# Attention and maxout kernel, batch 0: scores before row sums, the cast of v before the inverses, and four w2 transposes before the last values

## The chip, the cores and the metric

The kernel runs on one core of a Trainium2 chip. The metric is device time in microseconds (us) of one execution, as a median over runs. The engines have their own instruction queues and run side by side: TensorE (PE, with its weight loads shown as PEld), VectorE (DVE), ScalarE (ACT), GpSimd (POOL) and SyncE (SP). Each engine executes its own queue in order, and engines wait for one another on semaphores. Matmul results go to PSUM, which here is cut into four single banks and two pairs of banks.

## The reference

```python
def _attn_ref(q, k, v, E, F):                       # q, k, v: 8 x 8 x 1024 x 64; E, F: 64 x 1024
    k_proj = np.einsum('ks,bhsd->bhkd', E, k)
    v_proj = np.einsum('ks,bhsd->bhkd', F, v)
    scale = 1.0 / np.sqrt(q.shape[-1])
    scores = scale * np.matmul(q, k_proj.transpose(0, 1, 3, 2))
    scores = scores - np.max(scores, axis=-1, keepdims=True)
    attn = np.exp(scores)
    attn = attn / (np.sum(attn, axis=-1, keepdims=True) + 1e-09)
    return np.matmul(attn, v_proj)

def _moe_ref(x, w1, w2, w_out):                     # x: 8192 x 512; w1, w2: 512 x 1024; w_out: 1024 x 512
    h1 = x @ w1
    h2 = x @ w2
    g = np.maximum(h1, h2)
    return g @ w_out
```

The heads of the attention output are joined into x, and the second part runs on it. The kernel uses max(h1, h2) = relu(x (w1 - w2)) + x w2, so it needs the difference `wd_sb` = w1 - w2, and the product m = w2 w_out, for which w2 is transposed once (`w2t_sb`).

## The kernel before, in words

Work goes by batch (8 of them). In a batch k and v are projected to 64 rows per head, the scores of 8 heads are taken in four groups (g, j): g names four heads, j a half of the 512 positions that one tile holds. A group passes these steps, each a function that appends instructions to the engines' queues:

- `step_sc`: 16 score matmuls on PE (line 340) into a pair of banks, then one Exp on ACT (line 380) to `ex_sb`.
- `step_dn`: 8 matmuls with ones on PE (line 352), which write the row sums into the same pair of banks, then one Ln on ACT (line 388) to `ld_sb`.
- `step_inv`: one Exp(-x) on ACT (line 427), which turns the Ln into the inverse sums in place, and a small DMA of a few rows on SP's queue (line 396) for a later range check.
- `step_at`: 16 value matmuls on PE (line 352), and two products with the inverse on DVE (line 443), which write `xt_sb`.

`step_kv(..., "v")` projects v for some heads (line 195) and casts the result to `vp_sb` (line 207), on DVE or, for heads 4 to 8, on ACT. That last call takes two heads, then runs what is given as `between`, then takes the other two heads; both halves lie in one bank of a pair.

For batch 0 the second part has no saved sums yet. An up block (`up_slots`, line 525) is four accumulating matmuls of `wd_sb` with `xt_sb` into one single bank, then a relu on ACT or DVE. The blocks `u0[0]`, `u0[1]`, `u1[0]`, `u1[1]` are cut into a first half (`r1=2`, which needs only group g = 0) and a second half (`r0=2`, which needs g = 1); `u0` needs j = 0 and `u1` needs j = 1. `step_wd` (line 541) makes pieces of `wd_sb` on DVE. `step_w2t` turns 256 columns of w2 with eight transposes on PE (line 557) into one bank, and copies them to `w2t_sb` with ACT (line 563).

The order on every engine is the order of the calls (`tc.manual_schedule()`): nothing is moved by a scheduler. The four single banks are handed out in turn from the list `turn` (`mm_bank`); the two pairs alternate with each call of `att_banks`, so that each call waits until the pair of two calls ago has been read for the last time. The call of `att_banks()` alone only advances that alternation. The lines around the change are 979 to 1005 and the list `slots`, which orders the work after them.

In this order the pairs are taken so: scores (1,0) take a pair, which their row sums share; scores (1,1) take the other pair; v of heads 4 to 8 takes the first pair again; the values (1,0) take the first pair once more and the values (1,1) the second. The values (0,0) and (0,1) take the four single banks.

Of the kernel before, what the change touches and what calls it, by code (L numbers as in the profile page):

```python
# [10 lines left out]
FP16 = mybir.dt.float16  # L11
# [8 lines left out]
def kernel(  # L20
# [12 lines left out]
    nc = tc.nc  # L33
# [8 lines left out]
    NDC = DM // 128  # L42
# [20 lines left out]
    turn = [0, 1, 2, 3]  # L63

    def mm_bank(dtype=FP32, n=None):
        if n is None:
            n = turn.pop(0)
            turn.append(n)
        return ps.tile([128, 512 if dtype == FP32 else 1024], dtype, tag=f"mm{n}", name="mm_ps")

    def att_banks(dtype=FP32):
        return ps.tile(
            [128, 2, 512 if dtype == FP32 else 1024], dtype, tag="att", bufs=2, name="att_ps"
        )
# [108 lines left out]
    def step_kv(t, h0=0, h1=H, which="kv", att=False, dma=False, copy=nc.vector.tensor_copy, between=None):  # L183
        kv_ps = att_banks()[:, 0, :] if att else mm_bank(n=0 if dma else None)
        n = (h1 - h0) * D
        both = which == "v"
        nh = 2 if both else h1 - h0
        for h in range(0, h1 - h0, nh):
            if h and between is not None:
                between()  # L190
            for c in range(NC):
                for w in which:
                    i = "kv".index(w)
                    for r in range(2) if both else (i,):
                        nc.tensor.matmul(  # L195
                            out=kv_ps[r * KP : (r + 1) * KP, h * D : (h + nh) * D],
                            lhsT=eft[i][:, c, :],
                            rhs=t[w][:, h0 + h : h0 + h + nh, c, :],
                            start=(c == 0), stop=(c == NC - 1),
                        )  # L200
        zd = lambda ap: ap.rearrange("p (h d z) -> p h z d", d=D // 2, z=2)
        if "k" in which:
            eng = nc.vector.tensor_copy if which == "k" or dma else nc.scalar.copy
            kp = t["kp"][:, h0:h1]
            eng(out=kp[:, :, 0, :], in_=kv_ps[0:KP, 0:n].rearrange("p (h d) -> p h d", d=D))
        if both:
            copy(out=t["vp"][:, h0:h1], in_=zd(kv_ps[:, 0:n]))
        elif "v" in which:
            def finish_v():
                nc.vector.tensor_copy(out=t["vp"][KP:128, h0:h1], in_=zd(kv_ps[KP:128, 0:n]))  # L210
                if dma:
                    nc.vector.tensor_copy(out=kp[:, :, 1, :], in_=kp[:, :, 0, :])
                    step_kpt_dma(t)
                else:
                    step_vp(t, h0, h1)

            if att:
                return finish_v
            finish_v()


    def step_vp(t, h0=0, h1=H):
        fl = lambda ap: ap[:, h0:h1].rearrange("p h z d -> p (h z d)")
        nc.vector.tensor_copy(out=fl(t["vp"][0:KP]), in_=fl(t["vp"][KP:128]))
# [71 lines left out]
    def step_kpt_dma(t):  # L296
        nc.sync.dma_start_transpose(
            out=t["kpt"], in_=t["kp"].rearrange("p h r d -> p (h r d)")
        )
# [33 lines left out]
    def score(t, g, j, banks):  # L333
        for h in range(2):
            for o in range(2):
                for e in range(2):
                    head = 4 * g + 2 * h + e
                    for s in range(2):
                        pos = D * (o ^ e) + s * Z
                        nc.tensor.matmul(  # L340
                            out=banks[e][pos : pos + Z, h * W : (h + 1) * W],
                            lhsT=kpt_of(t, head, o)[:, s * Z : (s + 1) * Z],
                            rhs=t["qt"][o * D : (o + 1) * D, head, j * W : (j + 1) * W],
                            start=True, stop=True,
                        )
        t["ex", g, j] = soft.tile([128, 2, HALF], FP16, tag="soft", name="ex_sb")
# [12 lines left out]
    def sums_into(t, g, j, dn_ps):  # L359
        tiles_into(lambda o: dn_ps[:, o, :], t["ex", g, j], lambda rows, hh: ones16[rows, 0:Z])  # L360

    def values_into(t, g, j, at_ps):
        for z in range(2):
            tiles_into(
                lambda o: at_ps[o][:, z * W : (z + 1) * W], t["ex", g, j],
                lambda rows, hh: vp_of(t, 4 * g + hh, rows, z),
            )

    def new_xt(t):
        t["xt"] = xpool.tile([128, NP2, 2, HALF], FP16, tag="xt", name="xt_sb")  # L370

    def x_out(t, g, j):
        return t["xt"][:, 2 * g : 2 * g + 2, :, j * W : (j + 1) * W]


    def step_sc(t, g, j):
        sc_ps = att_banks()
        t["ps", g, j] = sc_ps
        score(t, g, j, [sc_ps[:, e, :] for e in range(2)])
        nc.scalar.activation(out=t["ex", g, j], in_=sc_ps, func=ACTF.Exp, scale=scale)  # L380

    def step_dn(t, g, j):
        dn_ps = t.pop(("ps", g, j))[:, :, 0:W]
        sums_into(t, g, j, dn_ps)
        ld = (ppool.tile([128, 2, W], FP32, tag="pd", bufs=4, name="ld_sb") if t is tiles[0]
              else soft.tile([128, 2, W], FP32, tag="soft", name="ld_sb"))
        t["ld", g, j] = ld
        nc.scalar.activation(out=t["ld", g, j], in_=dn_ps, func=ACTF.Ln)  # L388
# [4 lines left out]
    def check(inv):  # L393
        rows = checked[4 * n_checked[0] : 4 * n_checked[0] + 4, :]
        n_checked[0] += 1
        nc.sync.dma_start(
            out=rows, in_=inv.rearrange("(a z) o w -> a z (o w)", z=Z)[:, 0, :]
        )
# [26 lines left out]
    def step_inv(t, g, j):  # L425
        ld = t["ld", g, j]
        nc.scalar.activation(out=ld, in_=ld, func=ACTF.Exp, scale=-1.0)
        check(ld)

    def step_at(t, g, j, att=False, between=None):  # L430
        if "xt" not in t:
            new_xt(t)
        ld = t.pop(("ld", g, j))
        if att:
            both = att_banks()
            at_ps = [both[:, o, :] for o in range(2)]
        else:
            at_ps = [mm_bank() for _ in range(2)]
        values_into(t, g, j, at_ps)
        for o in range(2):  # L440
            if o and between is not None:
                between()
            nc.vector.tensor_tensor(
                out=x_out(t, g, j)[:, :, o, :],
                in0=at_ps[o].rearrange("q (z n) -> q z n", z=2),
                in1=ld[:, o, None, :].broadcast_to([128, 2, W]),
                op=ALU.mult,
            )
# [101 lines left out]
                out=rows(wd_sb), in0=rows(w1_sb), in1=rows(w2_sb), op=ALU.subtract  # L550
            )

    def step_w2t(f0, att=False):
        ps_t = att_banks(FP16)[:, 0, :] if att else mm_bank(FP16)
        for f in range(2):
            for r in range(NDC):
                nc.tensor.transpose(
                    out=ps_t[:, (f * NDC + r) * 128 : (f * NDC + r + 1) * 128],
                    in_=w2_sb[:, r, f0 + f * 128 : f0 + (f + 1) * 128],
                    identity=ident16,  # L560
                )
        fb = f0 // 128
        nc.scalar.copy(
            out=w2t_sb[:, fb : fb + 2, :].rearrange("q f m -> q (f m)"), in_=ps_t
        )
# [390 lines left out]
    t = tiles[0]  # L956
# [27 lines left out]
    step_sc(t, 1, 0)  # L984
    step_kv(t, 0, 2, "v")
    step_kv(t, 2, 4, "v")
    step_dn(t, 1, 0)
    step_sc(t, 1, 1)
    step_at(t, 0, 0)
    step_at(t, 0, 1)  # L990
    step_inv(t, 1, 0)
    step_kv(t, 4, 8, "v", True, copy=nc.scalar.copy, between=lambda: step_dn(t, 1, 1))
    step_inv(t, 1, 1)
    att_banks()
    for f0 in (0, 128):
        step_wd(f0, 0, 2, 128)
    step_at(t, 1, 0, True)
    u0, u1 = [*up_slots(t, 0)], [*up_slots(t, 1)]
    step_wd(0, 2, 4)
    step_at(t, 1, 1, True)  # L1000
    first_banks = turn[0:2], turn[2:4]
    for i in range(2):
        for u in u0, u1:
            u[i](r1=2)
    step_w2t(0, True)


    load_all(tiles[1], 1, "k", k)
# [4 lines left out]
    def loads(b, *names):  # L1013
# [15 lines left out]

    slots = [  # L1030
        (0, lambda: u0[0](r0=2)), (1, lambda: u0[1](r0=2)), (None, lambda: loads(1, "v", "q", "k")),
        (None, lambda: step_w2t(256, True)),
        (2, lambda: u1[0](r0=2)), (3, lambda: u1[1](r0=2)),
        (None, wd[1]), (4, u0[2]), (5, u0[3]),
        (None, wd[2]), (6, u1[2]), (7, u1[3]), (None, wt[2]), (None, wt[3]), (8, u0[4]), (9, u0[5]), (None, wd[3]),
# [45 lines left out]
    t = tiles[1]  # L1081
# [29 lines left out]
    t = tiles[2]  # L1111
# [8 lines left out]
    for b in range(3, B):  # L1120
        t = tiles[b]
        n = 2 * b - 3
# [13 lines left out]
    for i, (new, old) in enumerate(zip([*groups[1:], none], groups)):  # L1136
        n, h = divmod(i + 2, 2)
# [9 lines left out]
    for n, (b, o) in enumerate(units):  # L1147
        u = U[b, o]
# [33 lines left out]
    for key, slot in slots:  # L1182
        r = slot()
        pending = [g for g in [r, *(f() for f in pending)] if g is not None]
        for s in steps.pop(key, ()):
            r = s()
# [177 lines left out]
```

## Time and profile before

| | us |
|---|---|
| median of three runs (lowest, highest) | 319.72 (319.67, 319.75) |
| the profiled execution, its own time | 320.29 |
| its span in the trace | 318.5 |
| PE busy | 311.8 (98% of the span) |
| DVE busy | 241.1 (76%) |
| ACT busy | 206.0 (65%) |
| POOL busy | 41.4 (13%) |

A row of the timeline reads: start and duration in us, engine, line, operation, destination and source, shape, count; in brackets the idle time of the engine before it and what ended it. Rows of matmuls include the time that the last one needs to pass through the array, so rows that follow each other overlap. A row of the waits reads: engine, destination and line that waited, what it waited for, then total us, times, and longest. Times of the trace count from the start of the span.

### The profile page before, as it was taken

How to read it: one execution, taken by the hardware profiler on the slowest of the kernel's cores; microseconds unless marked ns; L12 is line 12 of the kernel's file. 1: busy time of each engine (PE TensorE's matmuls, PEld its weight loads, DVE VectorE, ACT ScalarE, POOL GpSimd, SP SyncE). 2: the span in 40 equal slices, each digit the busy share in tenths (PEclk: the TensorE clock that was granted, in tenths of full speed). 3: DMA queues.
4: the chain of work that ended last, by engine and by line, in shares of the span. 5: the costliest groups of instructions: out<-in, count | busy, mean ns of one | idle time of the engine just before them, and what ended most of it. 6: DMA issues, size and time to landing. Idle time of an engine off the chain costs nothing.

```text
span 318.5 us, 9309 instructions
## 1 busy us (share of the span) xinstructions
PE 311.8 (98%) x3922; PEld 253.8 (80%) x3922; DVE 241.1 (76%) x442; ACT 206.0 (65%) x373; POOL 41.4 (13%) x63
## 2 busy tenths in 40 slices
PE   7999999999999999999999999999999999999996
PEld 3565588888887888788887888788887888888885
DVE  2366889887969696896969696996969696969883
ACT  2386742777776777477776777477776777765541
POOL 8259102004000300012000400030000000000000
PEclk9999999999999999999999999999999999999999
DMA  7999999999989999799999999989979131313124
GB/s 179 206 202 197 207 207 201 207 156 141 204 163 183 171 209 245 208 188 147 225 229 219 169 199 245 221 155 174 230 153 217 42 101 36 102 35 102 36 99 136
DMA packets 76684, 53.71 MB, mean 169 GB/s; under 512 B 29664, under 2 KB 76128, under 8 KB 76640
## 3 DMA queue, kind: packets, MB, share of 16 engines
q0 software_dynamic: 30688, 28.05, 56.0%
q1 hardware_dynamic: 45664, 24.85, 33.1%
q8 instruction: 31, 0.51, 0.6%
q10 hardware_dynamic: 288, 0.20, 0.2%
q14 instruction: 13, 0.11, 0.1%
HBM read 57.15 MB, written 16.78 MB: 232 GB/s over the span
## 4 chain that ended last, share of the span: by engine, by line
PE 95%; DMA 3%; ACT 1%; DVE 1%; issue 0%; POOLq 0%
PE mm_ps L838 47%; PE mm_ps L746 27%; PE mm_ps L525 4%; PE mm_ps L195 4%; PE att_ps L352 4%; PE mm_ps L340 2%; DMA k_sb<-in_k_dram 2%; PE mm_ps L634 2%; PE att_ps L237 1%; PE mm_ps L311 1%; PE mm_ps L153 1%; DMA out_dram<-o_sb 1%; PE att_ps L340 0%; DVE qt_sb L316 0%; ACT ld_sb L388 0%
## 5 line engine op out<-in xcount | busy, mean ns | idle before, releaser
L720 ACT COPY p_sb<-mm_ps 128x512 f32<-128x512 f32 x179 | 101.7, 592 | 49.2 <-PE mm_ps L746 27.3
L838 PEld LDWEIGHTS <-big 128*128 128x128 f16 x768 | 73.5, 98 | 11.8 <-issue 3.6
L838 PE MATMUL mm_ps<-T_sb,big 128*128 128x256 f16 x576 | 76.9, 273 | 0.0
L761 DVE TENSOR_TENSOR gt_sb<-mm_ps,p_sb 128x512 f16<-128x512 f32 x56 | 38.5, 688 | 43.0 <-PE mm_ps L746 41.6
L746 PE MATMUL mm_ps<-big,big 128*128 128x256 f16 x336 | 50.4, 273 | 0.0
L746 PEld LDWEIGHTS <-big 128*128 128x128 f16 x448 | 43.8, 98 | 5.1
L838 PE MATMUL mm_ps<-wo_sb,gt_sb 128*128 128x256 f16 x256 | 42.6, 273 | 0.0
L838 PEld LDWEIGHTS <-gt_sb 128*128 128x128 f16 x376 | 35.7, 98 | 6.7 <-issue 2.7
L469 ACT ACTIVATE ex_sb<-mm_ps 128x512 f16<-128x512 f32 x50 | 27.2, 597 | 18.0 <-PE mm_ps L340 12.3
L746 PEld LDWEIGHTS <-wd_sb 128*128 128x128 f16 x336 | 32.9, 98 | 3.8
L746 PE MATMUL mm_ps<-xt_sb,wd_sb 128*128 128x256 f16 x224 | 32.8, 273 | 0.0
L499 DVE TENSOR_TENSOR xt_sb<-att_ps,ld_sb 128x1024 f16<-128x1024 f32 x26 | 31.7, 1219 | 0.2
L303 POOL COPY junk<-qt_sb 1x1 f16<-1x1 f16 x6 | 2.6, 432 | 172.3 <-DMA qt_sb<-q_sb 172.3
L838 PE MATMUL mm_ps<-m_sb,xt_sb 128*128 128x256 f16 x128 | 24.4, 273 | 0.0
L869 DVE TENSOR_TENSOR o_sb<-mm_ps,p_sb 128x512 f32<-128x512 f32 x32 | 21.9, 683 | 2.8 <-ACT p_sb L898 2.0
L764 DVE TENSOR_SCALAR gt_sb<-gt_sb 128x512 f16<-128x512 f16 (+1 forms) x60 | 20.9, 348 | 2.1
L706 DVE TENSOR_TENSOR big<-gt_sb 128x1024 f16<-128x1024 f16 x32 | 21.9, 683 | 0.0
L838 PE MATMUL mm_ps<-wo_sb,big 128*128 128x256 f16 x128 | 21.5, 273 | 0.0
L807 ACT ACTIVATE gt_sb<-mm_ps 128x512 f16<-128x512 f32 x28 | 16.8, 601 | 5.7 <-PE mm_ps L746 5.7
L838 PE MATMUL mm_ps<-T_sb,gt_sb 128*128 128x256 f16 x120 | 20.3, 273 | 0.0
L838 PEld LDWEIGHTS <-xt_sb 128*128 128x128 f16 x188 | 18.3, 98 | 2.3 <-issue 0.2
L761 DVE TENSOR_TENSOR gt_sb<-p_sb 128x512 f16<-128x512 f32 x28 | 19.1, 682 | 0.6 <-ACT p_sb L720 0.6
(121 smaller groups left out, 434.8 us busy)
## 6 DMA issues: line engine op xcount, KB each, us to landing
out_dram<-o_sb SPq DMA_DIRECT2D x62, 256.0 KB
k_sb<-in_k_dram POOLq DMA_DIRECT2D x7, 1024.0 KB, 9.7
v_sb<-in_v_dram POOLq DMA_DIRECT2D x7, 1024.0 KB, 15.4
q_sb<-in_q_dram POOLq DMA_DIRECT2D x5, 1024.0 KB, 22.8
q_sb<-in_q_dram POOLq DMA_DIRECT2D x6, 512.0 KB, 15.9
big<-in_moe_w_dram POOLq DMA_DIRECT2D x12, 128.0 KB, 6.4
v_sb<-in_v_dram POOLq DMA_DIRECT2D x4, 256.0 KB, 14.0
wo_sb<-in_moe_w_out_dram POOLq DMA_DIRECT2D x1, 1024.0 KB, 10.4
```

The source lines that it names most:

```text
L195: nc.tensor.matmul(out=kv_ps[r * KP : (r + 1) * KP, h * D : (h + nh) * D], lhsT=eft[i][:, c, :], rhs=t[w][:, h0 + h : h0 + h + nh, c, :], ...
L352: nc.tensor.matmul(out=dst(r ^ (hh % 2))[hh * Z : (hh + 1) * Z, :], lhsT=weights(rows, hh), rhs=ex[rows, hh % 2, hh // 2 * W : (hh // 2 + ...
L469: nc.scalar.activation(out=t["ex", g, j][:, e, :], in_=banks[e], func=ACTF.Exp, scale=scale)
L499: nc.vector.tensor_tensor(out=x_out(t, g, j).rearrange("q z o n -> q o z n"), in0=at_ps.rearrange("q o (z n) -> q o z n", z=2), in1=ld[:, ...
L706: nc.vector.tensor_tensor(out=S(i), in0=S(0) if x is None else x, in1=y(), op=op)
L720: copy(out=x, in_=bank)
L746: nc.tensor.matmul(out=bank[:, m * W : (m + 1) * W], lhsT=w_[:, n_, (2 * d + m) * 128 : (2 * d + m + 1) * 128], rhs=a[:, n_, :], start=(n ...
L761: nc.vector.tensor_tensor(out=c_blk(j, c), in0=two(x), in1=two(y), op=ALU.add)
L764: nc.vector.tensor_scalar_max(ap, ap, 0.0)
L807: nc.scalar.activation(out=out, in_=in_, func=ACTF.Relu)
L838: nc.tensor.matmul(out=bank[i][:, 0:CH] if two_banks else bank[:, i * CH : (i + 1) * CH], lhsT=a(c)[:, i * 128 : (i + 1) * 128], rhs=w_(c) ...
L869: nc.vector.tensor_tensor(out=o_sb, in0=two(x), in1=two(y), op=ALU.add)
```

## The change

Five things are changed, all in batch 0.

1. `step_sc(t, 1, 1)` comes ahead of `step_dn(t, 1, 0)`, on PE and so on ACT too.
2. `step_inv(t, 1, 0)` comes after the call that projects v of heads 4 to 8, so that ACT takes Ln (1,1) and the cast of v ahead of both inverses.
3. The first w2 transposes are split: four of them (rows r = 0 and 1) come ahead of the values (1,0), the other four (r = 2 and 3) stay where the eight were.
4. Their bank is no longer one of a pair but the second single bank in `turn`, which the fourth up block (`u1[1]`) takes later; `turn` is permuted, so that `u0[0]` and `u1[0]` keep their banks and `u0[1]` and `u1[1]` change theirs with each other.
5. The first half of `u1[1]`, whose bank now holds the transposes, moves from before those transposes to after the next eight (`step_w2t(256, True)`), ahead of the second half of `u1[0]`.

```diff
-    def step_w2t(f0, att=False):
-        ps_t = att_banks(FP16)[:, 0, :] if att else mm_bank(FP16)
+    def turn_w2(ps_t, f0, rs):
         for f in range(2):
-            for r in range(NDC):
+            for r in rs:
                 nc.tensor.transpose(
...
+    def step_w2t(f0, att=False, ps_t=None, rs=range(4)):
+        if ps_t is None:
+            ps_t = att_banks(FP16)[:, 0, :] if att else mm_bank(FP16)
+        turn_w2(ps_t, f0, rs)
...
     step_kv(t, 2, 4, "v")
+    step_sc(t, 1, 1)
     step_dn(t, 1, 0)
-    step_sc(t, 1, 1)
     step_at(t, 0, 0)
     step_at(t, 0, 1)
+    step_kv(t, 4, 8, "v", True, copy=nc.scalar.copy, between=lambda: step_dn(t, 1, 1))
     step_inv(t, 1, 0)
-    step_kv(t, 4, 8, "v", True, copy=nc.scalar.copy, between=lambda: step_dn(t, 1, 1))
     step_inv(t, 1, 1)
     att_banks()
+    w2t_bank = mm_bank(FP16, n=turn[1])
+    turn_w2(w2t_bank, 0, (0, 1))
...
     step_at(t, 1, 1, True)
+    turn[:] = [turn[i] for i in (0, 3, 2, 1)]
     first_banks = turn[0:2], turn[2:4]
-    for i in range(2):
-        for u in u0, u1:
-            u[i](r1=2)
-    step_w2t(0, True)
+    for u in u0[0], u1[0], u0[1]:
+        u(r1=2)
+    step_w2t(0, ps_t=w2t_bank, rs=(2, 3))
...
-        (None, lambda: step_w2t(256, True)),
+        (None, lambda: step_w2t(256, True)), (None, lambda: u1[1](r1=2)),
```

No instruction is added or removed: every engine has as many as before. DMA issues keep their order on SP and POOL; the small DMA of the inverse (1,0) goes with it.

## The prediction

> **What bounds the kernel now.** I read the page first: the busy times, the chain that ended last, and the granted clock.
>
> ```profile
> span 318.5 us, 9309 instructions
> PE 311.8 (98%) x3922; PEld 253.8 (80%) x3922; DVE 241.1 (76%) x442; ACT 206.0 (65%) x373; POOL 41.4 (13%) x63
> PEclk9999999999999999999999999999999999999999
> PE 95%; DMA 3%; ACT 1%; DVE 1%; issue 0%; POOLq 0%
> ```
>
> PE is busy for 98% of the span, at full granted clock, and carries 95% of the chain. So the change is worth what it does to PE's few gaps. The waits of PE from 18 to 60 us, and then from 60 us to the end, say where they are:
>
> ```profile
> PE att_ps L352 <- ACT vp_sb L207: 0.5, 1, 0.5
> PE att_ps L352 <- ACT ex_sb L380: 0.3, 1, 0.3
> ...
> PE mm_ps L1196 <- DMA out_dram<-o_sb: 1.2, 1, 1.2
> ```
>
> Two waits, 0.8 us together, both in the stretch that is edited. Nothing waits behind it until the last store. Whatever PE loses or wins before about 27 us therefore reaches the end nearly whole: no later gap can take it up. The chain in order of time shows what PE waited for:
>
> ```profile
> 20.36 0.60 ACT ld_sb L388
> 20.95 0.91 ACT ex_sb L380
> 21.87 0.52 ACT ld_sb L427
> 22.38 0.50 ACT ld_sb L388
> ```
>
> From 20.36 us on ACT sets the pace: Ln (1,0), Exp of scores (1,1), inverse (1,0), Ln (1,1), then the cast of v. The change rearranges just this queue. The timeline gives the steps, PE first:
>
> ```profile
> 18.43 0.41 PE L340 MATMUL att_ps<-qt_sb,kpt_sb 64*32 64x256 f16 x16
> 18.77 1.27 PE L195 MATMUL mm_ps<-v_sb,eft 128*64 128x128 f16 x32
> 19.98 0.30 PE L352 MATMUL att_ps<-ex_sb,ones 64*32 64x256 f16 x8
> 20.09 0.41 PE L340 MATMUL att_ps<-qt_sb,kpt_sb 64*32 64x256 f16 x16
> 20.31 0.74 PE L352 MATMUL mm_ps<-ex_sb,vp_sb 64*32 64x256 f16 x32
> 20.98 0.50 PEld L195 LDWEIGHTS <-eft 128*64 128x64 f16 x16 [0.21 <-issue]
> 21.00 0.64 PE L195 MATMUL att_ps<-v_sb,eft 128*64 128x128 f16 x16
> 21.92 0.30 PE L352 MATMUL att_ps<-ex_sb,ones 64*32 64x256 f16 x8 [0.28 <-ACT ex_sb L380]
> 22.15 0.64 PE L195 MATMUL att_ps<-v_sb,eft 128*64 128x128 f16 x16
> 23.25 0.63 PE L352 MATMUL att_ps<-ex_sb,vp_sb 64*32 64x256 f16 x32 [0.47 <-ACT vp_sb L207]
> 23.82 1.90 PE L525 MATMUL mm_ps<-xt_sb,wd_sb 128*128 128x512 f16 x8
> 25.55 0.61 PE L557 MATMUL att_ps<-ident,big 128*128 128x128 f16 x8
> 26.00 1.03 PE L525 MATMUL mm_ps<-xt_sb,wd_sb 128*128 128x512 f16 x4
> 26.86 0.61 PE L557 MATMUL att_ps<-ident,big 128*128 128x128 f16 x8
> 27.31 4.48 PE L525 MATMUL mm_ps<-xt_sb,wd_sb 128*128 128x512 f16 x20
> ```
>
> and ACT and DVE beside it:
>
> ```profile
> 18.91 1.02 ACT L380 ACTIVATE ex_sb<-att_ps 128x1024 f16<-128x1024 f32 x1 [0.57 <-PE att_ps L340]
> 20.36 0.60 ACT L388 ACTIVATE ld_sb<-att_ps 128x512 f32<-128x512 f32 x1 [0.42 <-PE att_ps L352]
> 20.85 1.02 ACT L380 ACTIVATE ex_sb<-att_ps 128x1024 f16<-128x1024 f32 x1
> 21.75 0.63 ACT L427 ACTIVATE ld_sb<-ld_sb 128x512 f32<-128x512 f32 x1
> 22.29 0.60 ACT L388 ACTIVATE ld_sb<-att_ps 128x512 f32<-128x512 f32 x1
> 22.83 0.37 ACT L207 CAST vp_sb<-att_ps 128x256 f16<-128x256 f32 x1
> 23.10 0.63 ACT L427 ACTIVATE ld_sb<-ld_sb 128x512 f32<-128x512 f32 x1
> 26.20 1.01 ACT L563 COPY big<-att_ps 128x1024 f16<-128x1024 f16 x1 [2.47 <-PE att_ps L557]
> ...
> 23.37 0.48 DVE L541 TENSOR_TENSOR wd_sb<-big,big 128x256 f16<-128x256 f16 x2
> 23.81 1.29 DVE L443 TENSOR_TENSOR xt_sb<-att_ps,ld_sb 128x512 f16<-128x512 f32 x2
> 25.02 0.42 DVE L541 TENSOR_TENSOR wd_sb<-big,big 128x512 f16<-128x512 f16 x1
> 25.35 1.28 DVE L443 TENSOR_TENSOR xt_sb<-att_ps,ld_sb 128x512 f16<-128x512 f32 x2
> ```
>
> **The change part by part.** I follow PE through the new order, with the durations above. An instruction of ACT starts 0.07 us after the last matmul it needs (18.43 + 0.41 = 18.84, Exp at 18.91), PE starts 0.05 us after ACT (23.20, then 23.25), and ACT instructions in a row overlap by about 0.1 us (Ln at 20.36 to 20.96, Exp at 20.85).
>
> *Scores (1,1) first.* They take the place of the row sums behind v, at 19.98, and end at 20.39; Exp (1,1) runs 20.46 to 21.48, where it ran 20.85 to 21.87. A gain of 0.39 us for that Exp. The row sums (1,0) lose nothing on PE, since 8 + 16 matmuls pass in the same time in either order.
>
> *What is queued behind.* Ln (1,0) now stands behind that Exp on ACT: from 21.37 to 21.97, where it ended at 20.96. Who waits for it is decided by the banks. Row sums (1,0) lie in the first pair, and v of heads 4 to 8 is projected into the same pair, so its first matmul may start only when Ln (1,0) has read it. In the trace it started at 21.00, right behind that Ln, but there PE had only just finished the values and the change of form (0.21 us of issue): the wait cost nothing. Now v can start only at 22.01, a full 1.01 us later, with PE standing still from 21.05. This is the term that decides.
>
> *From v to the values (1,0).* The first 16 matmuls of v take 0.58 us until the next row sums can start: 22.59, against 21.92. The old 0.28 us wait for Exp (1,1) is gone, long over at 21.48. From the row sums on, the pitch is the old one: v again at +0.23 (22.82), done at 23.46; Ln (1,1) from 22.96; the cast, 0.54 us behind the start of Ln and 0.04 behind v, whichever is later, 23.50 to 23.87; the values (1,0) at 23.92. Against 23.25 that is +0.67 us.
>
> *The inverse (1,0) behind the cast.* It saves nothing: before, the cast started at 22.83, and v had ended at 22.79, so it waited for v. Instead it makes the inverse late: it runs 23.77 to 24.40, where it was done at 22.38. DVE's products (1,0) need it, and start at 24.45 rather than 23.81. Behind them on DVE is the piece of `wd_sb` for the second halves: 1.21 us after the start of the products, 25.66 to 26.08, where it was 25.02 to 25.44. The check's small DMA goes with the inverse; SP has nothing else to issue there, and no engine waits for it soon.
>
> *Four transposes ahead of the values.* Eight took 0.45 us of PE from 25.55 to 26.00, so four are 0.23 us. They fall into the wait for the cast, between 23.46 and 23.92, where the bank (values (0,0), read by DVE) has been free since about 22.3 and the columns of w2 are there, as the `wd_sb` pieces at 23.37 used them without a wait. Gain 0.23 us; the bounds are 0 (cover gone) and 0.33 us (four of eight weight loads that take 0.65 us).
>
> *The up blocks.* After the values, the first halves start 0.57 us on, at 24.49; six matmuls of 0.216 us (23.82 to 25.55 for eight) bring PE to 25.79, four transposes to 26.02. The second half of `u0[0]` then needs the `wd_sb` piece of 26.08: PE starts at 26.13. That is a new wait of 0.10 us, where there was 0.5 us of slack before. Then four matmuls (0.86), eight transposes (0.45) and the two moved matmuls of `u1[1]` (0.43) bring the second half of `u1[0]` to 27.87, against 27.31. Moving these two costs nothing: their bank is read by the 1.01 us ACT copy of the first transposes, 26.24 to 27.25, and PE comes to them at 27.44; if that copy were over 0.15 us later they would wait. Products (1,1) end at 27.3, in time for 27.87.
>
> The sum: +0.67 (values later) - 0.23 (transposes hidden) + 0.10 (wait for `wd_sb`), and with rounding 27.87 - 27.31 = **+0.56 us**. Bounds by the same rows: scores at 19.90, as the last weight load of v is done at 19.88, or at 20.09, with a change of form like the 0.21 us above, give -0.08 and +0.11; the wait for `wd_sb` 0 to 0.2. Together +0.35 to +0.85. The profiled execution took 320.29 us (span 318.5), 0.57 above the median of the runs shown, 319.72; the difference carries over, so 320.85 in such an execution and **320.3** as a median. A measurement of this kernel can tell about 0.2%, 0.64 us, from no change: I forecast no measurable change, on the slow side.
>
> **The rivals.**
>
> *Slower, the transposes lose their cover.* PE pays for a change between matmul forms (the 0.21 us of issue at 20.98). The four transposes put one more such change between v (128x64) and the values (64x32). If they start 0.2 us after v's end, at 23.66, the last ends at 24.04 (0.61 us for eight, less four of 0.056), and the values start there and not at 23.92: it decides from 0.1 us on. The values are then at +0.79 or more, products follow PE rather than the inverse (24.04 + 0.41 + 0.07, so 24.52), and the second halves start at 26.20: +0.63 to +0.75 with a later scores start, 320.4. TensorEngine Tiling (Key Properties) of the Trainium skill says that changing the tiling mode drains TensorE; by that rule each switch waits for the pass through the array, and the sum would be 320.4 rather than 320.3. The 0.21 us agrees with it. Against it: the 0.46 us gap before the cast holds nearly all of it.
>
> *Not slower, the bank does not hold v.* If v started at 21.0 as before, row sums (1,1) would follow at 21.58, v again when its last heads have landed (it started at 22.15), say 22.0, the cast at 22.68 and the values at 23.10. Then products (1,0) start at 23.81 behind the `wd_sb` pieces of 23.37, as before, the second halves at 25.49, and `u1[0]` at 27.23: -0.08 us, 319.6. Even so DVE holds the gain back, so over 0.64 us faster needs something outside this stretch. Against it: the banks of a pair alternate by the order of the calls, which is unchanged here.
>
> *The clock falls.* PE's standing still grows from 0.2 to about 1 us around 21.5, near the gap before the values. A stretch of 3.4 us at half clock would cost 1.7 us: 322. Against it:
>
> ```profile
> 7.00:10.50 3.50, 2.46 (x19) 1.78 (x17) 0.82 (x3) 0.03 (x1) 1.40 (x2) 1.00 1.24 212
> ```
>
> In this stretch of 3.5 us PE (the first busy time) was idle for 1.04 us and the clock stayed at 1.00. TensorE: Matmul & The Clock Gate of the Trainium skill (A second HAM failure mode) tells of frequent micro-idles that made the clock swing, which speaks against any new gap; this row does not bear it out at such a share.
>
> **How the numbers follow.** The likeliest case, up to +0.64, has 0.48. Over +0.64, from the upper end of my bounds and the lost cover, has 0.41; the fallen clock 0.02. The bank that does not hold has 0.04, within 0.2%, and 0.05 is left for a gain from elsewhere that I do not see. So faster 0.05, the same 0.52, slower 0.43. The range takes the bounds, 320.07 to 320.57, and 0.25 us more on each side, since the 0.57 us between one execution and the median is itself known from one profile: 319.8 to 320.8. It leaves out the clock, the bank and the unseen gain, 0.11. The likeliest case's own range is 320.05 to 320.4.
>
> **What would show it.** Right: Exp (1,1) at about 20.5 with Ln (1,0) behind it; v of heads 4 to 6 at 22.0 with PE waiting about 1 us for `ld_sb`, line 388; no wait of row sums (1,1) for Exp; values (1,0) near 23.9; four transposes just ahead of them; a short wait for `wd_sb` near 26.1; 20 up matmuls' stretch about 0.5 us later than before. Wrong: v at 21.0, values before 23.3, or a later gap of PE that grows or shrinks.

## The result

The changed kernel takes 320.35 us (median of 16 runs, 320.15 to 320.99) against 319.86 us for the kernel before in the same comparison (16 runs, 319.45 to 320.36). The ratio is 1.0017, with a 95% interval of 1.0009 to 1.0025: 0.54 us slower by the ratio, 0.29 to 0.80 by its interval. The ratio is inside the 0.2% that was named as the bound of no change, on its slow side; the interval leaves out zero and reaches a little past that bound. Ratios here and below leave out the few executions that the chip ran in a slow state, the medians do not, so the two can differ a little.

The profiled executions hide this. Both spans are 318.5 us. The reason is ahead of the change: in the profile of after the batch 0 stretch begins 0.66 us earlier, because the first loads landed earlier in that execution (PE waited 1.0 us for k in the profile of before, and not at all for k in that of after). So all places below are counted from A, the first matmul behind v of heads 2 to 4 (19.98 us in the profile of before, 19.32 in that of after).

PE in the timeline of the changed kernel:

```profile
19.32 0.41 PE L340 MATMUL att_ps<-qt_sb,kpt_sb 64*32 64x256 f16 x16
19.55 0.29 PE L352 MATMUL att_ps<-ex_sb,ones 64*32 64x256 f16 x8
19.66 0.74 PE L352 MATMUL mm_ps<-ex_sb,vp_sb 64*32 64x256 f16 x32
21.36 0.64 PE L195 MATMUL att_ps<-v_sb,eft 128*64 128x128 f16 x16 [0.96 <-ACT ld_sb L388]
21.93 0.30 PE L352 MATMUL att_ps<-ex_sb,ones 64*32 64x256 f16 x8
22.16 0.64 PE L195 MATMUL att_ps<-v_sb,eft 128*64 128x128 f16 x16
22.73 0.40 PE L556 MATMUL mm_ps<-ident,big 128*128 128x128 f16 x4
23.27 0.63 PE L352 MATMUL att_ps<-ex_sb,vp_sb 64*32 64x256 f16 x32
23.83 1.47 PE L525 MATMUL mm_ps<-xt_sb,wd_sb 128*128 128x512 f16 x6
25.14 0.39 PE L556 MATMUL mm_ps<-ident,big 128*128 128x128 f16 x4
25.50 1.04 PE L525 MATMUL mm_ps<-xt_sb,wd_sb 128*128 128x512 f16 x4
26.38 0.61 PE L556 MATMUL att_ps<-ident,big 128*128 128x128 f16 x8
26.82 4.91 PE L525 MATMUL mm_ps<-xt_sb,wd_sb 128*128 128x512 f16 x22
```

The fourth row is the new wait: 0.96 us for line 388, the Ln of row sums (1,0). ACT in the same stretch shows why, and the weight loads and DVE show the rest:

```profile
19.80 1.02 ACT L380 ACTIVATE ex_sb<-att_ps 128x1024 f16<-128x1024 f32 x1 [1.08 <-PE att_ps L340]
20.72 0.59 ACT L388 ACTIVATE ld_sb<-att_ps 128x512 f32<-128x512 f32 x1
22.31 0.60 ACT L388 ACTIVATE ld_sb<-att_ps 128x512 f32<-128x512 f32 x1 [0.99 <-PE att_ps L352]
22.84 0.37 ACT L207 CAST vp_sb<-att_ps 128x256 f16<-128x256 f32 x1
23.11 1.15 ACT L427 ACTIVATE ld_sb<-ld_sb 128x512 f32<-128x512 f32 x2
...
23.27 0.35 PEld L352 LDWEIGHTS <-vp_sb 64*32 64x32 f16 x32 [0.31 <-ACT vp_sb L207]
...
23.82 1.29 DVE L443 TENSOR_TENSOR xt_sb<-att_ps,ld_sb 128x512 f16<-128x512 f32 x2 [0.59 <-ACT ld_sb L427]
25.03 0.41 DVE L541 TENSOR_TENSOR wd_sb<-big,big 128x512 f16<-128x512 f16 x1
```

Ln (1,0) runs at 20.72, right behind Exp (1,1), and v starts 0.05 us after it ends at 21.31. The waits of PE from 18 us on, and the granted clock in 40 slices of the span, in tenths, from the page:

```profile
PE att_ps L195 <- ACT ld_sb L388: 1.0, 1, 1.0
PE mm_ps L195 <- DMA v_sb<-in_v_dram: 0.5, 2, 0.3
...
PE mm_ps L1202 <- DMA out_dram<-o_sb: 1.2, 1, 1.2
...
PEclk9999999999999999999999999999999999999999
```

The old waits for the cast and for Exp (1,1), 0.8 us together, are gone from this list, and one of 1.0 us stands in their place (the waits for `v_sb` lie ahead of A). What is left of the wait for the cast shows at the weight loads of the values, 0.31 us. Behind it there is again nothing until the last store. The mean granted clock of the execution was 1.000.

The places in all kernels, in us from A (the last column is the span less A; a kernel in which two matmuls of `u1[1]` come first has `u1[0]` 0.43 us behind the start of that row):

| kernel | A | v of heads 4 to 6 | values (1,0) | products (1,0) | second half u0[0] | second half u1[0] | span - A |
|---|---|---|---|---|---|---|---|
| before | 19.98 | 1.02 | 3.27 | 3.83 | 6.02 | 7.33 | 298.5 |
| before, second look | 19.54 | 1.02 | 3.27 | 3.83 | 6.02 | 7.33 | 298.6 |
| predicted for after | 19.98 | 2.03 | 3.94 | 4.47 | 6.15 | 7.89 | |
| after | 19.32 | 2.04 | 3.95 | 4.50 | 6.18 | 7.93 | 299.2 |
| after, second look | 19.73 | 2.05 | 3.95 | 4.51 | 6.19 | 7.94 | 299.2 |
| scores first only | 19.52 | 2.05 | 3.96 | 4.51 | 6.70 | 8.01 | 299.2 |
| scores back | 19.50 | 1.03 | 3.28 | 3.84 | 5.51 | 7.26 | 298.5 |
| v in a single bank | 19.50 | 1.75 | 3.65 | 4.20 | 5.88 | 7.63 | 298.8 |
| inverse back | 19.58 | 2.05 | 3.96 | 4.51 | 6.19 | 7.94 | 299.1 |
| cut wd_sb piece | 19.62 | 1.02 | 3.27 | 3.83 | 5.37 | 7.12 | 298.4 |
| cut wd_sb piece, again | 19.38 | 1.03 | 3.28 | 3.84 | 5.38 | 7.13 | 298.3 |
| wd_sb pieces early | 19.38 | 1.02 | 5.68 | 6.23 | 8.12 | 9.65 | 300.8 |

From A to `u1[0]` the change costs 7.93 - 7.33 = 0.60 us, and from A to the end 0.6 to 0.7.

### The profile page after: what moved, and what is told of

It is laid out like the page before. It is cut to its first block, busy times and chain, and to the rows that moved or that the text cites. A ratio compares the mean times of both kernels' runs of the same rounds, so it can differ in the third digit from the quotient of the medians.

```text
span 318.5 us, 9308 instructions
## 1 busy us (share of the span) xinstructions
PE 311.9 (98%) x3922; PEld 253.8 (80%) x3922; DVE 241.2 (76%) x442; ACT 206.3 (65%) x373; POOL 39.9 (13%) x63
## 4 chain that ended last, share of the span: by engine, by line
PE 92%; DMA 5%; POOL 1%; ACT 1%; issue 0%; DVE 0%; POOLq 0%
PE mm_ps L842 47%; PE mm_ps L750 27%; PE mm_ps L525 4%; DMA v_sb<-in_v_dram 4%; PE att_ps L352 3%; PE mm_ps L195 3%; PE mm_ps L340 2%; PE mm_ps L638 2%; PE att_ps L237 1%; DMA out_dram<-o_sb 1%; PE mm_ps L311 1%; POOL k_sb L108 0%; POOL q_sb L108 0%; PE att_ps L340 0%; PE mm_ps L556 0%; ACT ld_sb L388 0%
## 5 line engine op out<-in xcount | busy, mean ns | idle before, releaser
L303 POOL COPY junk<-qt_sb 1x1 f16<-1x1 f16 x6 | 1.5, 246 | 174.4 <-DMA qt_sb<-q_sb 174.4
```

## The experiments

**Two second looks.** Does the stretch behind A keep its shape while A moves?

> The kernel before, a second look. If A moves between executions with the landing of the loads and the rest does not, A differs from 19.98 and v of heads 4 to 6 (A + 1.02), values (A + 3.27) and u1[0] (A + 7.33) hold to 0.05 us.

> The changed kernel, a second look. As for the kernel before: A may differ from 19.32; v at A + 2.04, values at A + 3.95 and u1[0] at A + 7.93 hold to 0.05 us.

Single executions took 319.86 (before) and 320.73 us (after). PE in the second look of before, then of after:

```profile
18.97 0.64 PE L195 MATMUL mm_ps<-v_sb,eft 128*64 128x128 f16 x16 [0.39 <-DMA v_sb<-in_v_dram]
19.54 0.30 PE L352 MATMUL att_ps<-ex_sb,ones 64*32 64x256 f16 x8
```

```profile
18.38 1.42 PE L195 MATMUL mm_ps<-v_sb,eft 128*64 128x128 f16 x32 [0.30 <-DMA v_sb<-in_v_dram]
19.73 0.41 PE L340 MATMUL att_ps<-qt_sb,kpt_sb 64*32 64x256 f16 x16
```

A moved by 0.44 us in one and 0.41 in the other, with the landing of the loads: in the second look of before PE waited 0.39 us for v just ahead of A, where the first look has no wait for v but one of 1.0 us for k. Every place behind A held to 0.01 us in both pairs. So a difference of 0.6 us behind A can be read from one profile of each kernel here, and not from a pair of spans.

**The scores first, alone.**

```diff
-    step_dn(t, 1, 0)
     step_sc(t, 1, 1)
+    step_dn(t, 1, 0)
```

> The kernel before with only scores (1,1) ahead of row sums (1,0). Times from A, the first matmul behind v of heads 2 to 4; before: v of heads 4 to 6 at A + 1.02, values (1,0) at A + 3.27, second half of u1[0] at A + 7.33; after: 2.04, 3.95, 7.93. Theory (v waits for Ln (1,0), now behind Exp (1,1)): v at A + 2.04, values at A + 3.95, u1[0] at A + 8.01, so about 0.68 us slower than before, more than the whole change. Rival (an earlier Exp (1,1) helps, and what costs is the late inverse or the split transposes): v at A + 1.0, u1[0] at A + 6.9 to 7.3, not slower than before.

It took 320.54 us against 319.88, ratio 1.0021 (1.0012 to 1.003). PE:

```profile
21.57 0.64 PE L195 MATMUL att_ps<-v_sb,eft 128*64 128x128 f16 x16 [0.96 <-ACT ld_sb L388]
...
23.48 0.63 PE L352 MATMUL att_ps<-ex_sb,vp_sb 64*32 64x256 f16 x32 [0.47 <-ACT vp_sb L207]
```

v at A + 2.05, `u1[0]` at A + 8.01, the theory's numbers. This swap alone has the whole loss, and the old wait for the cast is still there beside the new one. The rival falls: an earlier Exp (1,1) bought nothing.

**The scores back, the rest kept.**

```diff
-    step_sc(t, 1, 1)
     step_dn(t, 1, 0)
+    step_sc(t, 1, 1)
```

> The changed kernel with row sums (1,0) ahead of scores (1,1) again; the other parts stay. Theory: v at A + 1.02, values at A + 3.27, four transposes hidden ahead of them, second halves held by the piece of wd_sb until A + 5.5, u1[0] at A + 7.25: 0.08 us faster than before, 0.6 us faster than the changed kernel. Rival (the inverse behind the cast or the transposes cost time): values later than A + 3.35 or u1[0] later than A + 7.4, so slower than before.

It took 319.72 us against 319.88, ratio 0.9998 (0.9989 to 1.0007): the time can't be told from no change, and 0.6 us under the changed kernel. PE:

```profile
22.25 0.40 PE L556 MATMUL mm_ps<-ident,big 128*128 128x128 f16 x4
22.78 0.63 PE L352 MATMUL att_ps<-ex_sb,vp_sb 64*32 64x256 f16 x32
```

The transposes fit ahead of the values without moving them (A + 3.28), and `u1[0]` comes at A + 7.26, 0.07 before the old place. The other parts together are a small gain, held back by DVE: `u0[0]` at A + 5.51 waits for its `wd_sb` piece, 0.14 us behind the end of the transposes.

**v in a single bank.** The scores stay ahead, but v no longer shares the pair of the row sums.

```diff
...
+        kv_ps = (mm_bank(n=n_bank) if n_bank is not None else
+                 att_banks()[:, 0, :] if att else mm_bank(n=0 if dma else None))
-        kv_ps = att_banks()[:, 0, :] if att else mm_bank(n=0 if dma else None)
...
-    step_kv(t, 4, 8, "v", True, copy=nc.scalar.copy, between=lambda: step_dn(t, 1, 1))
+    step_kv(t, 4, 8, "v", True, copy=nc.scalar.copy, between=lambda: step_dn(t, 1, 1), n_bank=turn[0])
...
-    att_banks()
```

> The changed kernel with v of heads 4 to 8 in a single bank, the one that the first product (0,0) on DVE has read, and not in the pair that holds row sums (1,0). Scores stay ahead. Theory (the shared pair is what makes v wait): v starts behind that product, A + 1.75, values at A + 3.66, u1[0] at A + 7.63: 0.3 us faster than the changed kernel, 0.3 us slower than before. Rival (it is the order on PE or the queue on ACT itself, whatever the bank): v at A + 2.04 and values at A + 3.95 as in the changed kernel.

It took 320.15 us against 319.88, ratio 1.0007 (0.9998 to 1.0016). PE, whose line 195 is line 196 here, and the waits of PE:

```profile
21.25 0.64 PE L196 MATMUL mm_ps<-v_sb,eft 128*64 128x128 f16 x16 [0.67 <-DVE xt_sb L444]
...
PE mm_ps L196 <- DVE xt_sb L444: 0.7, 1, 0.7
```

With another bank v waits for that bank's last reader, a product on DVE, and starts at A + 1.75. The values keep their pairs (the call of `att_banks()` alone goes, as v takes none), and the 0.30 us reach `u1[0]` whole. So the shared pair is what ties v to Ln (1,0).

**The inverse (1,0) back ahead of v**, in the changed kernel.

```diff
+    step_inv(t, 1, 0)
     step_kv(t, 4, 8, "v", True, copy=nc.scalar.copy, between=lambda: step_dn(t, 1, 1))
-    step_inv(t, 1, 0)
```

> The changed kernel with the inverse (1,0) ahead of v of heads 4 to 8 again, as before the change; scores ahead and transposes ahead stay. Times from A, the first matmul behind v of heads 2 to 4; changed kernel: values (1,0) at A + 3.95, products (1,0) on DVE at A + 4.50, second half of u1[0] at A + 7.93. Theory (ACT is idle for 1 us while v waits, so the inverse fits there and delays nothing): values at A + 3.95, products follow the values at A + 4.43, u1[0] at A + 7.86, 0.07 us faster than the changed kernel, 0.5 us slower than before. Rival (the inverse ahead of the cast holds ACT up): values later than A + 4.1, slower than the changed kernel.

It took 320.5 us against 319.9, ratio 1.0019 (1.0004 to 1.0034). ACT and DVE:

```profile
21.61 0.63 ACT L427 ACTIVATE ld_sb<-ld_sb 128x512 f32<-128x512 f32 x1
22.57 0.60 ACT L388 ACTIVATE ld_sb<-att_ps 128x512 f32<-128x512 f32 x1 [0.33 <-PE att_ps L352]
...
24.09 1.29 DVE L443 TENSOR_TENSOR xt_sb<-att_ps,ld_sb 128x512 f16<-128x512 f32 x2 [0.59 <-ACT ld_sb L427]
```

Neither expectation held in full. ACT is not held up, as the theory said, but the 0.07 us did not come: the inverse (1,0) was done at 22.24, 1.85 us before the products, and they still began 0.55 us behind the values (23.54), exactly as in the changed kernel (23.27 and 23.82). The profile's name for what ended DVE's wait, line 427, is that of the other inverse, which happens to end just then (23.38 and 0.63 us, so 24.01); the products (1,0) do not use it. What is left is the values on PE. The products (0,0) bear this out: in the changed kernel their inverses were long done, and they start at 20.35, 0.69 us behind the start of the values (0,0).

**Pieces of `wd_sb` early, and an up block into the gap**, in the kernel before.

```diff
     step_sc(t, 1, 1)
+    for f0 in (0, 128):
+        step_wd(f0, 0, 2, 128)
     step_at(t, 0, 0)
...
-    for f0 in (0, 128):
-        step_wd(f0, 0, 2, 128)
+    u0, u1 = [*up_slots(t, 0)], [*up_slots(t, 1)]
+    first_banks = turn[0:2], turn[2:4]
+    u0[0](r1=2)
     step_at(t, 1, 0, True)
...
```

> The kernel before with the first two pieces of wd_sb ahead of the products (0,0) on DVE, into 0.6 us that DVE is idle, and the first half of u0[0] ahead of the values (1,0), into PE's wait for the cast; scores, inverses, transposes as before. Theory (PE is the bound, and work put into its gaps comes off the end if DVE is not late): values at A + 3.35 to 3.45, second half of u0[0] at A + 5.75 without a wait, u1[0] at A + 7.06: 0.27 us faster than before. Rival (DVE is late with the products (0,0), or the change of form ahead of the values costs what the gap gives): u1[0] at A + 7.3 or later.

It took 323.34 us against 319.88, ratio 1.012 (1.0104 to 1.0135): 3.8 us slower, where 0.27 us faster was expected. DVE, then PE:

```profile
22.77 0.49 DVE L541 TENSOR_TENSOR wd_sb<-big,big 128x256 f16<-128x256 f16 x2 [2.99 <-DMA big<-in_moe_w_dram]
23.18 2.48 DVE L443 TENSOR_TENSOR xt_sb<-mm_ps,ld_sb 128x512 f16<-128x512 f32 x4
...
24.52 0.60 PE L525 MATMUL mm_ps<-xt_sb,wd_sb 128*128 128x512 f16 x2 [2.34 <-DVE xt_sb L443]
```

The weights w1 and w2 land only by 22.77 us. DVE stood 2.99 us in front of them, with the products (0,0) behind it in the queue, and PE waited 2.34 us for those. The rival named DVE, but not this cause. What I had taken for idle time of DVE was idle before data that was not there. The trace accounts for 2.3 us of the loss (`u1[0]` at A + 9.65 against A + 7.33). The profiled execution took 322.02 us at a granted clock of 1.000; the other three took 323.30 to 324.42 us at 0.989 to 0.995, while none of the 27 executions of the kernel before beside them was under 0.998. So the rest of the loss went with a lower clock. That the standstill of 2.34 us brought it about is not shown: none of those three was traced, and single executions of the kernel before, in other comparisons, had 0.989 and 0.995 as well.

**The `wd_sb` piece cut in two**, with the scores back and the other parts kept; timed twice.

```diff
-    step_wd(0, 2, 4)
+    for f0 in (0, 128):
+        step_wd(f0, 2, 4, 128)
```

> Row sums (1,0) ahead of scores (1,1) again, the other parts of the change stay, and the wd_sb piece behind the products (1,0) is cut into two of 128 columns, so that u0[0] waits for the first alone. Theory (with the scores back, DVE is what holds the second half of u0[0]): it starts at A + 5.35 to 5.40 and not at A + 5.51, u1[0] at A + 7.10 to 7.15: about 0.2 us faster than the kernel before. Rival (something else holds u0[0]): A + 5.5 again, time as without the cut, 0.06 us under the kernel before.

> The same kernel as with the cut wd_sb piece, timed again, since its interval (0.9986 to 1.0021) could not tell 0.2 us. By its trace (u1[0] at A + 7.12 against A + 7.33 before) the ratio is 0.9994 and the time about 0.2 us under the kernel before. Rival: the gain is lost behind A + 7.12, and the ratio is 1.0000 or more.

It took 319.81 us against 319.9 (ratio 1.0004, 0.9986 to 1.0021), and again 319.96 against 320.2 (0.9994, 0.9965 to 1.0023). PE in the first of them:

```profile
24.76 0.39 PE L556 MATMUL mm_ps<-ident,big 128*128 128x128 f16 x4
24.99 1.04 PE L525 MATMUL mm_ps<-xt_sb,wd_sb 128*128 128x512 f16 x4
```

`u0[0]` follows the transposes after 0.23 us, without a wait, and `u1[0]` comes at A + 7.12, 0.21 us before its old place; the span from A on is 298.4 (298.3 in the second) against 298.5 and 298.6. So the trace shows the gain in place, while both intervals are too wide to say that the kernel is faster than the one before.

## Why the prediction was right

The forecast was 320.3 us, +0.56, no change on the slow side; measured were 320.35 us, +0.54 by the ratio, and 0.60 us in the trace. By its steps:

- *Scores (1,1) first, Exp 0.39 us earlier.* Held: Exp at A + 0.48 as forecast, where it was A + 0.87. Worth nothing, as forecast: this Exp was over before v could start.
- *What is queued behind.* Held, and shown from both sides: v at A + 2.04 (forecast 2.03), with the swap alone giving the whole loss, its undoing the whole return, and another bank moving v to the release of that bank.
- *From v to the values.* Held: +0.68 us against +0.67, by the table.
- *The inverse behind the cast.* That it saves nothing held: with the inverse back, the kernel has the same places to 0.01 us. That it is what makes the products late did not hold. The inverse was as late as forecast (done at 23.74), and the products began where the step put them (4.50, forecast 4.47), but with the inverse early they begin there too: they wait 0.55 us from the start of the values, a wait that the profile of before hid, since DVE was then busy with the `wd_sb` pieces until the same moment. The prediction had this path only in a rival, priced at 0.48 us (0.41 and 0.07). So the number came out by luck: two chains that both hang on the cast end within 0.1 us of each other.
- *Four transposes ahead.* Held: they run at 22.73 to 23.13, and the weights of the values still wait 0.31 us for the cast behind them. The rival of the lost cover is refuted: the change of form from v to the transposes cost nothing that shows (v ends at 22.80, they start at 22.73), where that rival had them start 0.2 us behind v's end. With the scores back and the `wd_sb` piece cut in two, so that the second halves wait for nothing, `u1[0]` comes 0.21 us earlier than in the kernel before, for the 0.23 us forecast.
- *The up blocks.* The wait for the `wd_sb` piece is 25.50 less 25.37 (25.14 and four of 0.056 us), 0.13 us, for 0.10 forecast. The moved matmuls of `u1[1]` did not wait for the copy. The measured terms add up to 0.68 - 0.23 + 0.13 = 0.58 us.
- *The rival of the clock* did not come true: the mean granted clock was 0.999 or 1.000 in all 16 executions, with a standstill of 0.96 us in the profiled one. *The rival of the bank that does not hold* is refuted by the first row of waits.

Three things were thinner than the prediction said. The w2 columns that "are there" were there by about 0.7 us: in the changed kernel their load landed at about 22.0 us and the transposes began at 22.73. (The wait of DVE until 22.77 in the run that asked early was for w1, whose load landed 0.7 us behind that of w2.) The bounds that its sum names, -0.08 and +0.11 for the scores and 0 to 0.2 for the `wd_sb` wait, give +0.38 to +0.77, not the +0.35 to +0.85 that it states; the measured cost lies in both. And the 0.57 us between the profiled execution and the median was no constant to carry over: it was mostly the late A of that execution (19.98, where a second look had 19.54 and took 319.86 us). It did no harm, because the sum was a difference. That the cost counts as no measurable change was close: 0.54 us lies near the bound of 0.64 us, and the prediction gave 0.43 to the other side.

## What to carry to other kernels

Before moving an instruction ahead on an engine, list what stands behind it in that queue, and for each the buffer that it frees and who takes that buffer next: here an Exp moved ahead delayed a Ln, the Ln held a pair of banks, and the next matmuls into that pair stood 0.96 us. Idle time of an engine in a trace is free only if its operands have landed by then; look for the landing, not for the gap. And compare two traces from a common event behind the loads, not from the start.

## What was not expected of the hardware

The point at which the loads let the stretch begin moved between 19.32 and 19.98 us over these executions of nearly the same program, while the places behind it repeated to 0.01 us where a kernel was profiled twice. A difference of 0.6 us in a 318.5 us span was invisible in the two spans, and plain in the places behind A.
